# A fused pooled-attention and MLP kernel: three places of the first batch's order are changed

## The chip, the cores and the metric

The kernel runs on one core of a Trainium2 chip. The metric is the device time of one execution in microseconds (us); five runs of the kernel before are given, and their median is the time that a change is measured against. Beside it stands one execution taken by the hardware profiler, with its own time.

## The reference

Two stages are computed, one after the other. The first is attention over pooled keys and values (batch 8, heads 8, sequence 576, head size 64; eight neighbouring keys are averaged into one, so there are 72). The second is an MLP block with a mix over tokens in front.

```python
k_p = k.reshape(B, H, Sp, pool, D).mean(axis=3)        # pool = 8, Sp = 72
v_p = v.reshape(B, H, Sp, pool, D).mean(axis=3)
scores = scale * np.matmul(q, k_p.transpose(0, 1, 3, 2))
attn = softmax(scores)
x = np.matmul(attn, v_p)                               # then heads side by side: (8, 576, 512)

a1 = alpha1 * x + beta1
tok = np.einsum('ts,bsd->btd', w_tok, a1)
u = x + lam * tok
a2 = alpha2 * u + beta2
ch = np.maximum(a2 @ w_ch1, 0.0) @ w_ch2               # 512 -> 2048 -> 512
out = u + lam * ch
```

## The kernel before, in words

Each batch passes through attention (`att_...`), the token mix (`mix_T`, `mix_uT`) and the MLP (`mlp_A`, `mlp_B`). From the second batch on, attention of batch b+1 is interleaved with the MLP of a block of four 128-token chunks by due times that are sorted in a loop (L712 to L747). The first batch has nothing to lie beside: its attention is written out by hand from L583 to L662, and this is the stretch that the change touches. Every engine carries out its own instructions in the order in which the program issues them, so a line's place in this list is its place in its engine's queue.

The first batch in order:

- `keep_warm(4)` (L584) runs four matmuls on a constant tile ahead of everything else on TensorE. Two `broadcast`s (L267) spread lam and lam*alpha1 over the partitions; ScalarE copies them out (L586, L588).
- `cast_q` (L130), `att_F` (L369, L373): q is cast to bf16, transposed on TensorE and copied out. q and k come in two halves u of four heads, and the last 64 of the 576 tokens of all heads ("the rest") come in a tile of their own, `rem_raw`.
- `sum_k` (L138, L139) adds up k in three steps; the fourth level of the pooling is in a matmul. `cast_rem` (L121, L123, L124) casts the rest of q and adds up the rest of k into `rem_k`; before, all three instructions are on GpSimd. Its third argument, `copy`, gives the engine of the cast alone.
- `row_of_xs` (L273) writes one row of 512 products beta1*lam into `xs`, the right operand of the token mix: a bias row. It is one VectorE instruction on one partition. Only the fifth chunk of the mix's sum reads that row.
- `att_K` (L401, L404, L408): pooled keys by matmul, the third of them from `rem_k`, then two copies into `kpT`. `att_S` (L453, L455): scores of one head and their exponentials. `sum_v` (L416, L418), `att_V` (L424, L428): the same for v.
- `att_AV(0, h)` (L470 to L477): product of one head on TensorE; VectorE takes the reciprocal of the row sums and writes `x_tm`. `att_X` (L484, L488) multiplies two heads of `x_tm` by lam*alpha1 into `xs`, on GpSimd for the first six heads and on VectorE for the last two.
- In between the heads, `setup_wtok(c)` (L288, L291) transposes one column block of w_tok by five matmuls and ScalarE copies it into `wtT`; `setup_rowsum(c)` (L300, L302) sums its rows by five matmuls, and ScalarE copies one row. `setup_vectors` (L278) and `keep_warm(2)` follow.
- `mix_T(0, 0)` (L512) is the first product of the token mix. It reads all 512 columns of `xs`, so it follows all eight heads. After it TensorE has the mix and the MLP.

There are six PSUM buffers in turn for nearly all of TensorE's results (`gp`), and two more for the broadcasts and the MLP's sums. The loads are issued on SyncE's queue in the order q, k, rests, q, k, rest of v, v; w_tok and the MLP's weights are issued from GpSimd's queue, where `load_wtok` (L147, L149) and `load_w1` (L324) stand behind `cast_q(0, 1)` and the rest of v. The loads of the second batch are held back by a VectorE memset (L82) behind head 5's product, and GpSimd's part of v (`sum_v(0, 1)`) is held back by a memset (L613) that follows VectorE's `v_sum`.

Of the kernel before, what the change touches and what calls it, by code (L numbers as in the profile page):

```python
# [23 lines left out]
def kernel(  # L24
# [18 lines left out]
    nc = tc.nc  # L43
# [8 lines left out]
    def gp(name):  # L52
        return psA.tile([P, 512], FP, tag="gp", name=name)
# [10 lines left out]
    def keep_warm(count):  # L64

        ps = gp("ps_warm")
        for _ in range(count):
            nc.tensor.matmul(out=ps, lhsT=warm[:, 0:P], rhs=warm)
# [4 lines left out]
    def new_batch(b):  # L73
        st1[b] = {"qT": {}, "ET": [None] * H, "raw": [None] * 2, "q": [None] * 2,
                  "k": [None] * 2, "v": [None] * 2}
# [41 lines left out]
    def cast_rem(b, eng, copy=None):  # L117
        raw = st1[b]["rem_raw"]
        rq = work.tile([P, 4, D], BF, tag="rem_q", bufs=2, name="rem_q")
        rk = work.tile([P, 2, D], BF, tag="rem_k", bufs=2, name="rem_k")  # L120
        (copy or eng.tensor_copy)(out=rq, in_=raw[:, 0])  # L121
        t = raw[:, 1]
        eng.tensor_tensor(out=t[:, 0:2], in0=t[:, 0:2], in1=t[:, 2:4], op=ALU.add)  # L123
        eng.tensor_tensor(out=rk, in0=t[:, 0:1].to_broadcast((P, 2, D)),  # L124
                          in1=t[:, 1:2].to_broadcast((P, 2, D)), op=ALU.add)
        st1[b]["rem"] = rq, rk

    def cast_q(b, u, copy):
        bf = work.tile([P, 16, D], BF, tag="q_bf", bufs=3, name="q_bf")
        copy(out=bf, in_=st1[b]["raw"][u][:, 0].rearrange("p e j d -> p (e j) d"))  # L130
        st1[b]["q"][u] = bf

    def sum_k(b, u, eng):

        t = st1[b]["raw"][u][:, 1]
        bf = work.tile([P, 2, 2, D], BF, tag="k_bf", bufs=4, name="k_bf")
        for n in (4, 2):
            eng.tensor_tensor(out=t[:, :, 0:n], in0=t[:, :, 0:n], in1=t[:, :, n:2 * n], op=ALU.add)  # L138
        eng.tensor_tensor(out=bf, in0=t[:, :, 0:1].to_broadcast((P, 2, 2, D)),  # L139
                          in1=t[:, :, 1:2].to_broadcast((P, 2, 2, D)), op=ALU.add)  # L140
        st1[b]["k"][u] = bf
# [122 lines left out]
    def broadcast(i):  # L264

        ps = psB.tile([P, DM], FP, tag="ch", bufs=2, name="ps_bc")
        nc.tensor.matmul(out=ps, lhsT=ones_row, rhs=vecs[0:1, i])  # L267
        return ps

    def row_of_xs(i, eng):  # L270

        p0 = 64 - 64 * i
        eng.tensor_tensor(out=xs_pool[i][p0:p0 + 1, 4, :], in0=vecs[p0:p0 + 1, 2],  # L273
                          in1=vecs[p0:p0 + 1, 0], op=ALU.mult)
# [6 lines left out]
    def setup_wtok(tcx, copy):  # L281

        trc = P if tcx < 4 else REM
        w = wt_bf[0:trc, S * tcx:S * tcx + 640]
        strided = w[:, 0:512].rearrange("p (m c) -> p c m", c=4)
        ps_w = gp("ps_w").bitcast(BF)
        for sc in range(5):
            nc.tensor.transpose(out=ps_w[0:P, trc * sc:trc * sc + trc],  # L288
                                in_=strided[:, sc, :] if sc < 4 else w[:, 512:640],
                                identity=identity_bf[0:trc, 0:trc])  # L290
        copy(out=wtT[:, 0:5, P * tcx:P * tcx + trc],  # L291
             in_=ps_w[:, 0:5 * trc].rearrange("p (s t) -> p s t", t=trc))
# [84 lines left out]
    def att_Frem(b, us, copy):  # L377

        st = st1[b]
        if "ps_qr" not in st:  # L380
            ps_q = gp("ps_qr").bitcast(BF)
            ps_q = ps_q[:, 0:256].rearrange("p (a m) -> p a m", a=2)
            for a in range(2):
                nc.tensor.transpose(out=ps_q[:, a],
                                    in_=st["rem"][0][:, 2 * a:2 * a + 2].rearrange(
                                        "p j d -> p (j d)"),
                                    identity=identity_bf)
            st["ps_qr"] = ps_q
        for u in us:
            copy(out=qT_of(b, u)[:, :, 256:288].rearrange("p h (i a) -> p h i a", a=2),  # L390
                 in_=st["ps_qr"].rearrange("p a (i h) -> p h i a", h=8)[:, 4 * u:4 * u + 4])

    def att_K(b, u, *copies):

        st = st1[b]
        ps_kp = gp("ps_kp")


        kp = ps_kp[:, 0:320].rearrange("p (r h y) -> p r h y", r=2, h=2)
        for e in range(2):  # L400
            nc.tensor.matmul(out=kp[:, :, :, 8 + 32 * e:40 + 32 * e],  # L401
                             lhsT=st["k"][u][:, e].rearrange("p t d -> p (t d)"), rhs=sel_k)
        kp = ps_kp[:, 0:320].rearrange("p (r y) -> p r y", r=2)
        nc.tensor.matmul(out=kp[:, :, 72:88], lhsT=st["rem"][1].rearrange("p t d -> p (t d)"),  # L404
                         rhs=pool_rem[:, 4 * u:4 * u + 4])
        for j in range(2):
            rows = slice(64 * j, 64 * j + 64)
            copies[j % len(copies)](  # L408
                out=kpT_pool[u][rows, j].rearrange("p r (h x) -> p r h x", h=2)[:, :, :, 0:72],
                in_=kp[rows, :, 8:152].rearrange("p r (h x) -> p r h x", h=2))  # L410
# [35 lines left out]
    def att_S(b, h):  # L446

        st = st1[b]
        u, r, hh = h // 4, h // 2 % 2, h % 2
        ET, n = ET_pool[(8 * b + h) % 6], P if hh else SPG  # L450
        for j in range(2):
            ps_sc = gp("ps_sc")
            nc.tensor.matmul(out=ps_sc[0:n, 0:288], lhsT=kpT_pool[u][:, j, r, 72 * hh:72 * hh + n],  # L453
                             rhs=st["qT"][u][:, h % 4, :])
            nc.scalar.activation(out=ET[0:n, 64 + j:64 + S + j:2], in_=ps_sc[0:n, 0:288],  # L455
                                 func=AF.Exp, bias=0.0, scale=1.0 / 64)
        st["ET"][h] = ET

    def att_AV(b, h):
        st = st1[b]  # L460
        if "x" not in st:
            st["x"] = work.tile([P, 5, DM], FP, tag="x_tm", bufs=1, name="x_tm")
        hp, hh = h // 2, h % 2
        n = P if hh else SPG
        ET, vp1, x = st["ET"][h][0:n], vp1_pool[b % 2][hh][0:n, hp], st["x"]
        ps_av = gp("ps_av")
        av = ps_av[:, 0:5 * 66].rearrange("p (c x) -> p c x", x=66)
        for c in range(4):
            m0 = 64 + 256 * (c // 2) + c % 2
            nc.tensor.matmul(out=av[:, c, :], lhsT=ET[:, m0:m0 + 256:2], rhs=vp1)  # L470

        r0 = 576 - 64 * (b % 2)
        nc.tensor.matmul(out=av[:, 4, :], lhsT=ET[:, r0:r0 + 128], rhs=vp1)  # L473
        rec = work.tile([P, 5], FP, tag="rec", bufs=2, name="rec")
        nc.vector.reciprocal(out=rec, in_=av[:, :, 64:65])  # L475
        dd = D * h
        nc.vector.tensor_tensor(out=x[:, :, dd:dd + D], in0=av[:, :, 0:64],  # L477
                                in1=rec.unsqueeze(2).to_broadcast((P, 5, D)), op=ALU.mult)

    def att_X(b, h0, h1, eng=nc.vector):  # L480

        x, xs = st1[b]["x"], xs_pool[b % 2]
        cols = slice(D * h0, D * h1)
        eng.tensor_tensor(  # L484
            out=xs[:, 0:4, cols], in0=x[:, 0:4, cols],
            in1=lamal_bc[:, cols].unsqueeze(1).to_broadcast((P, 4, D * (h1 - h0))), op=ALU.mult)
        p0 = 64 * (b % 2)
        eng.tensor_tensor(out=xs[p0:p0 + 64, 4, cols], in0=x[p0:p0 + 64, 4, cols],  # L488
                          in1=lamal_bc[p0:p0 + 64, cols], op=ALU.mult)
# [91 lines left out]


    new_batch(1)  # L583
    keep_warm(4)  # L584
    ps_lam = broadcast(0)
    nc.scalar.copy(out=lam_bc, in_=ps_lam)  # L586
    ps_lamal = broadcast(1)
# [2 lines left out]
    att_F(0, 0)  # L590
    fill_E()
    sum_k(0, 0, nc.vector)
    cast_rem(0, nc.gpsimd)
    cast_q(0, 1, nc.gpsimd.tensor_copy)
    row_of_xs(0, nc.vector)
    att_Frem(0, (0,), nc.scalar.copy)
    att_K(0, 0, nc.vector.tensor_copy, nc.scalar.copy)
    att_Frem(0, (1,), nc.vector.tensor_copy)
# [7 lines left out]
    att_F(0, 1)  # L606
    att_S(0, 2)
    att_K(0, 1, nc.vector.tensor_copy)
    att_S(0, 3)
    v_00 = st1[0]["v"][0]  # L610
    sum_v(0, 0)
# [23 lines left out]
    load_v(1, 0)  # L635
    load_v(1, 1)
    att_X(0, 4, 6, nc.gpsimd)
    setup_wtok(2, nc.scalar.copy)
    att_AV(0, 6)
    setup_rowsum(0)  # L640
    setup_rowsum(1)
    setup_wtok(3, nc.scalar.copy)
    att_AV(0, 7)
    att_X(0, 6, 8)
    setup_rowsum(2)
    setup_rowsum(3)
# [131 lines left out]
```

The softmax here doesn't subtract the row's maximum and nothing guards it: scores larger than these inputs give would overflow.

## Time and profile before

| | |
|---|---|
| median of 5 runs | 370.13 us (370.0 to 371.06) |
| profiled execution | 370.5 us, of which the span from first to last instruction is 368.7 us |
| TensorE busy | 357.1 us, 97% of the span |
| VectorE, ScalarE, GpSimd busy | 218.4, 214.1, 126.2 us |
| chain of waits by engine | TensorE 91%, ScalarE 3%, DMA 2%, VectorE 1% |
| first product of the token mix starts | 25.34 us after the span's start |

In the profile PE is TensorE's matmul, PEld its weight load, DVE VectorE, ACT ScalarE, POOL GpSimd, and SP the engine that issues most of the loads. In the timeline a row gives start and duration in us, then engine, line, operation, output <- inputs, shape and count, and in brackets the idle time before it and what ended it. The chain of waits goes back from the last instruction to whatever released it, step by step; it is the list of what had to be done one after another. A queue's name with a q behind it (SPq) means that the engine issues a transfer.

### The profile page before, as it was taken

To read this page: it belongs to the slowest core of one execution; us is meant where nothing else is said; L and a number is where in the kernel's file an instruction comes from. 1 tells how busy PE (TensorE), PEld (TensorE's weight loads), DVE (VectorE), ACT (ScalarE), POOL (GpSimd) and SP (SyncE) were. 2 spreads that over 40 slices of the span, in tenths; PEclk is the share of its full clock that TensorE was granted. 3 is DMA by queue.
4 is the path that set the end of the run, shared out by engine and by line. 5 is a ranking of instruction groups with operands and counts; after the bars stand their busy time and mean duration, and the time that the engine had idled before them with its cause. 6 is when DMAs were issued, how large, how long until landed. Compare 5 with 4: busy or idle time off the path is not lost.

```text
span 368.7 us, 6142 instructions
## 1 busy us (share of the span) xinstructions
PE 357.1 (97%) x2304; PEld 197.9 (54%) x2346; DVE 218.4 (59%) x437; ACT 214.1 (58%) x420; POOL 126.2 (34%) x182
## 2 busy tenths in 40 slices
PE   7799999999999999999999999999999999999995
PEld 2477655455545554555455555555455545544544
DVE  7765544883786368734876387727863687543011
ACT  3855984389527970698158923895279705712710
POOL 7857813072507231542227140905072410000000
PEclk9999999999999999999999999999999999999999
DMA  7999993039012901192107402470100002002002
GB/s 241 274 232 322 245 296 106 24 127 349 30 42 85 341 16 51 57 306 80 59 28 254 162 30 57 159 256 30 56 30 2 29 31 57 2 28 85 2 28 85
DMA packets 19575, 43.27 MB, mean 117 GB/s; under 512 B 2193, under 2 KB 4565, under 8 KB 19546
## 3 DMA queue, kind: packets, MB, share of 16 engines
q1 hardware_dynamic: 17488, 37.89, 29.9%
q0 software_dynamic: 1888, 4.86, 6.8%
q8 instruction: 18, 0.29, 0.3%
q10 hardware_dynamic: 170, 0.14, 0.2%
q14 instruction: 11, 0.09, 0.1%
HBM read 38.30 MB, written 9.44 MB: 129 GB/s over the span
## 4 chain that ended last, share of the span: by engine, by line
PE 91%; ACT 3%; DMA 2%; DVE 1%; issue 1%; SPq 1%
PE ps_ch L566 33%; PE ps_h L543 32%; PE ps_tok L512 12%; PE ps_sc L453 4%; PE ps_av L470 2%; PE ps_uT L527 2%; DMA qk_raw<-in_k_dram 2%; ACT Hj L548 2%; PE ps_q L369 1%; PE ps_w L288 1%; SPq L84 1%; PE ps_av L473 1%; PE ps_kp L401 1%; PE ps_rs L300 0%; ACT qT L373 0%
## 5 line engine op out<-in xcount | busy, mean ns | idle before, releaser
L543 PE MATMUL ps_h<-u_fm,w 128*128 128x512 bf16 (+1 forms) x575 | 133.7, 373 | 1.4 <-ACT u_fm L529 0.4
L566 PE MATMUL ps_ch<-w,Hj 128*128 128x512 bf16 x489 | 123.9, 379 | 1.3 <-issue 0.2
L548 ACT ACTIVATE Hj<-ps_h,bias_cols 128x512 bf16<-128x512 f32 x144 | 97.1, 691 | 34.0 <-PE ps_h L543 33.5
L543 PEld LDWEIGHTS <-w 128*128 128x128 bf16 x592 | 64.1, 114 | 48.3 <-issue 0.6
L566 PEld LDWEIGHTS <-Hj 128*128 128x128 bf16 x592 | 55.6, 98 | 49.1 <-issue 0.2
L529 ACT COPY u_fm<-ps_uT 128x512 bf16<-128x512 bf16 x36 | 21.1, 588 | 80.5 <-PE ps_uT L527 80.4
L484 POOL TENSOR_TENSOR xs<-x_tm,lamal_bc 128x512 bf16<-128x512 f32 x24 | 30.5, 1272 | 82.3 <-DVE x_tm L477 82.3
L455 ACT ACTIVATE ET<-ps_sc 128x288 f16<-128x288 f32 (+1 forms) x128 | 51.6, 488 | 11.1 <-PE ps_sc L453 10.6
L512 PE MATMUL ps_tok<-xs,wtT 128*128 128x512 bf16 (+1 forms) x200 | 49.3, 379 | 0.1
L573 DVE TENSOR_TENSOR u_sb<-u_sb,ps_ch 128x512 f32<-128x512 f32 (+1 forms) x37 | 24.9, 673 | 24.9 <-PE ps_ch L566 23.8
L408 DVE CAST kpT<-ps_kp 64x288 bf16<-64x288 f32 x31 | 14.1, 455 | 40.3 <-PE ps_kp L404 40.0
L572 DVE TENSOR_TENSOR ps_ch<-lam_bc,ps_ch 128x512 f32<-128x512 f32 x32 | 22.2, 693 | 24.9 <-PE ps_ch L566 24.8
L514 DVE TENSOR_TENSOR u_sb<-x_tm,ps_tok 128x512 f32<-128x512 f32 (+1 forms) x40 | 27.4, 685 | 13.0 <-PE ps_tok L512 12.8
L477 DVE TENSOR_TENSOR x_tm<-ps_av,rec 128x320 f32<-128x320 f32 x64 | 31.5, 492 | 2.7
L475 DVE RECIPROCAL rec<-ps_av 128x5 f32<-128x5 f32 x64 | 12.3, 193 | 34.6 <-PE ps_av L473 34.4
L512 PEld LDWEIGHTS <-wtT 128*128 128x128 bf16 (+1 forms) x200 | 18.8, 98 | 23.4 <-DVE xs L484 2.0
L453 PE MATMUL ps_sc<-qT,kpT 128*128 128x288 bf16 (+1 forms) x128 | 29.3, 306 | 0.9 <-DVE kpT L408 0.8
L138 POOL TENSOR_TENSOR qk_raw<-qk_raw 128x512 f32<-128x512 f32 (+1 forms) x28 | 29.7, 1060 | 1.1
L516 DVE TENSOR_TENSOR u_bf<-u_sb,al_bc 128x512 bf16<-128x512 f32 (+1 forms) x39 | 27.3, 700 | 1.4
L671 POOL COPY ticks<-ticks 1x1 f32<-1x1 f32 x6 | 1.1, 178 | 73.4 <-DVE ticks L667 73.4
L470 PEld LDWEIGHTS <-ET 72*128 72x128 f16 (+1 forms) x256 | 17.1, 102 | 14.1 <-DVE vp L428 0.6
L416 DVE TENSOR_TENSOR v_u<-v_u 128x512 f32<-128x512 f32 (+1 forms) x30 | 23.5, 783 | 0.8
(115 smaller groups left out, 324.6 us busy)
## 6 DMA issues: line engine op xcount, KB each, us to landing
qk_raw<-in_q_dram SPq DMA_DIRECT2D x16, 512.0 KB, 7.1
qk_raw<-in_k_dram SPq DMA_DIRECT2D x16, 512.0 KB, 6.6
v_u<-in_v_dram SPq DMA_DIRECT2D x32, 256.0 KB, 7.2
out_dram<-u_sb SPq DMA_DIRECT2D x32, 256.0 KB, 2.3
w<-in_moe_w_ch_dram POOLq DMA_DIRECT2D x2, 1024.0 KB, 13.8
w<-in_moe_w_ch_dram POOLq DMA_DIRECT2D x4, 512.0 KB, 10.7
rem_raw<-in_q_dram SPq DMA_DIRECT2D x8, 128.0 KB, 4.7
rem_raw<-in_k_dram SPq DMA_DIRECT2D x8, 128.0 KB, 5.2
```

The lines of the kernel that those rows point to most:

```text
L138: eng.tensor_tensor(out=t[:, :, 0:n], in0=t[:, :, 0:n], in1=t[:, :, n:2 * n], op=ALU.add)
L453: nc.tensor.matmul(out=ps_sc[0:n, 0:288], lhsT=kpT_pool[u][:, j, r, 72 * hh:72 * hh + n], rhs=st["qT"][u][:, h % 4, :])
L455: nc.scalar.activation(out=ET[0:n, 64 + j:64 + S + j:2], in_=ps_sc[0:n, 0:288], func=AF.Exp, bias=0.0, scale=1.0 / 64)
L477: nc.vector.tensor_tensor(out=x[:, :, dd:dd + D], in0=av[:, :, 0:64], in1=rec.unsqueeze(2).to_broadcast((P, 5, D)), op=ALU.mult)
L484: eng.tensor_tensor(out=xs[:, 0:4, cols], in0=x[:, 0:4, cols], in1=lamal_bc[:, cols].unsqueeze(1).to_broadcast((P, 4, D * (h1 - h0))), op= ...
L512: nc.tensor.matmul(out=ps_tok, lhsT=wtT[0:kk, at, t0:t0 + P], rhs=xs[0:kk, sc, :], start=(sc == 0), stop=(sc == 4))
L514: nc.vector.tensor_tensor(out=s["u"][p0:p1, :], in0=st1[b]["x"][p0:p1, c, :], in1=ps_tok[p0:p1, 0:DM], op=ALU.add)
L516: eng.tensor_tensor(out=s["u_bf"][p0:p1, :], in0=s["u"][p0:p1, :], in1=al2_bc[p0:p1, :], op=ALU.mult)
L543: nc.tensor.matmul(out=ps_h[:, t0:t1], lhsT=w1_of(cc, j), rhs=u_fm[n][:, cc, t0:t1], start=(cc == 0), stop=(cc == 3))
L548: nc.scalar.activation(out=t, in_=ps_h, func=AF.Relu, bias=bias_cols[:, j:j + 1], scale=1.0)
L566: nc.tensor.matmul(out=ps, lhsT=Hj[n, j][:, 128 * m:128 * m + 128], rhs=w2_of(n, j, cols), start=(j == 0), stop=(j == NJ - 1))
L573: nc.vector.tensor_tensor(out=u, in0=u, in1=ps, op=ALU.add)
```

## The change

Four edits in the list of the first batch. `keep_warm(4)` at the start goes. `cast_rem(0)` keeps GpSimd for the cast of q's rest, and VectorE takes the two additions of k's rest, behind `sum_k(0, 0)`. `row_of_xs(0)` leaves its place ahead of the first half's `att_K` and goes behind the second half's, ahead of `sum_v(0, 0)`. The product of head 6 goes ahead of the transposes of w_tok's block 2, and that of head 7 goes ahead of two row sums and the transposes of block 3.

```diff
     new_batch(1)
-    keep_warm(4)
     ps_lam = broadcast(0)
...
     fill_E()
     sum_k(0, 0, nc.vector)
-    cast_rem(0, nc.gpsimd)
+    cast_rem(0, nc.vector, nc.gpsimd.tensor_copy)
     cast_q(0, 1, nc.gpsimd.tensor_copy)
-    row_of_xs(0, nc.vector)
     att_Frem(0, (0,), nc.scalar.copy)
     att_K(0, 0, nc.vector.tensor_copy, nc.scalar.copy)
...
     att_K(0, 1, nc.vector.tensor_copy)
+    row_of_xs(0, nc.vector)
     att_S(0, 3)
     v_00 = st1[0]["v"][0]
     sum_v(0, 0)
...
     att_X(0, 4, 6, nc.gpsimd)
+    att_AV(0, 6)
     setup_wtok(2, nc.scalar.copy)
-    att_AV(0, 6)
+    att_AV(0, 7)
     setup_rowsum(0)
     setup_rowsum(1)
     setup_wtok(3, nc.scalar.copy)
-    att_AV(0, 7)
     att_X(0, 6, 8)
     setup_rowsum(2)
     setup_rowsum(3)
```

## The prediction

> **What bounds the kernel now.** I read the page first, then the chain of waits of the first 40 us, then each engine's timeline there.
>
> ```profile
> PE 357.1 (97%) x2304; PEld 197.9 (54%) x2346; DVE 218.4 (59%) x437; ACT 214.1 (58%) x420; POOL 126.2 (34%) x182
> PE   7799999999999999999999999999999999999995
> PEclk9999999999999999999999999999999999999999
> ```
>
> TensorE is busy in all slices but the first two and the last, so after some 20 us a delay at the start is not won back, and a gain at the start is kept. The change touches only those first 26 us. The chain of waits there (start, us, what):
>
> ```profile
> 4.39 6.85 DMA qk_raw<-in_k_dram
> ...
> 12.45 0.84 DVE k_bf L139
> ...
> 13.34 0.39 PE ps_kp L401 x2
> ...
> 14.27 0.46 DVE kpT L408
> ...
> 14.77 0.70 DVE v_u L416
> ...
> 15.95 0.30 DVE v_sum L418
> ...
> 16.30 0.30 PE ps_v L424
> ...
> 16.62 0.29 DVE vp L428
> ...
> 16.96 0.40 PE ps_av L470 x4
> ...
> 23.56 0.70 ACT wtT L291
> ...
> 24.30 0.44 PE ps_rs L300 x5
> ...
> 24.89 0.32 PE ps_warm L68
> ...
> 25.34 3.41 PE ps_tok L512 x15
> ```
>
> Three parts are to be seen. Up to 11.24 the second k transfer decides. From there to 16.96 it is VectorE, back to back: k's sum, k's copies, v's sum, v's copy. From 16.96 to 25.34 it is TensorE, with one stop at the end, where the row sum of block 3 waits for ScalarE's copy of that block. The mix starts at 25.34; what this start gains or loses I carry to the end of the kernel, since no wait on a transfer stands between 11.3 and 60 us in the list of waits, by which the loss could be swallowed.
>
> The rows of VectorE and GpSimd that I use for costs:
>
> ```profile
> 9.16 0.83 DVE L273 TENSOR_TENSOR xs<-vecs 1x512 bf16<-1x512 f32 x1
> 10.02 0.45 DVE L408 CAST kpT<-ps_kp 64x288 bf16<-64x288 f32 x1
> 24.51 0.69 DVE L484 TENSOR_TENSOR xs<-x_tm,lamal_bc 128x512 bf16<-128x512 f32 x1
> 25.12 0.28 DVE L488 TENSOR_TENSOR xs<-x_tm,lamal_bc 64x128 bf16<-64x128 f32 x1
> 9.41 1.48 POOL L130 CAST q_bf<-qk_raw 128x1024 bf16<-128x1024 f32 x1
> ```
>
> **The change part by part.**
>
> *The bias row behind k's copies.* At its old place the row (9.16 to 9.99) stands in the gap that ends with the transfer: VectorE idles 0.60 us before 11.26. Its new place is between k's last copy (ends 14.73) and v's sum (14.77), where VectorE has no gap. All of it goes on the chain. Cost, start to start: an elementwise product of 512 columns with an independent one behind it takes 25.12 - 24.51 = 0.61 us (L484 to L488). Lower bound 0.55 (L262, one partition, 4.71 to the next start at 5.26), upper bound 0.83 (the row itself at 9.16, beside GpSimd's work). At 14.8 GpSimd issues weight loads (13.93 to 15.48) and reads no tile, so I take 0.61. Behind it wait v's sum, the matmul L424, GpSimd's memset L613 and with it the second half of v, and all products: +0.61. The loads of batch 1 (memset L82, then eleven issues on SP's queue) come 0.61 later too; their first user, GpSimd's cast at 31.27, starts without a wait behind its own work, which has moved as far.
>
> *Rests of k on VectorE.* Two additions (L123, L124) of 128 columns leave GpSimd (0.51 each) and stand behind `k_bf` (ends 9.13). A VectorE sum with such an output takes 0.29 (L418 at 15.95). Two dependent ones: 9.15 + 0.31 + 0.31, so `rem_k` is there at about 9.75 instead of 9.43; the matmul L404 takes 0.21 (9.49 to 9.70 before), so k's first copy can start at 10.02. Before, it started at 10.02 as well, held not by the matmul but by the bias row on VectorE. So one delay takes another's place: 0. GpSimd disturbs this, though. Its cast of q's second half (1.48) moves up to 1.02 earlier, if that q has landed, and may run beside the two sums. The row at 9.16 shows what that does: L273 took 0.83 beside this cast against 0.61 alone (L262), +0.21. The page "SBUF — State Buffer" of the Trainium skill, section "Who interferes with whom", says more: a VectorE instruction with two SBUF inputs and a GpSimd instruction that reads SBUF exclude each other for a whole instruction. By that the sums could wait 1.48 for the cast, and k's first copy would be at about 11.4. I keep to the row: up to +0.2 for each sum. The cover is thin: TensorE's work behind that copy ends at 13.22, and the second `att_K` starts at 13.34, so 0.12 us of lateness is free and the rest counts. Between -0.12 (GpSimd's rest-of-v sums, also earlier, leave the 0.83 of L139 at 12.45 undisturbed, which gains only until TensorE is free) and +0.3; I take 0.
>
> *GpSimd's queue.* Behind the cast are two issues of w_tok, three sums of v's rest and two issues of w1; they move earlier by at most 1.02 and then stop at the memset L613, which waits for v's sum in either order. w_tok takes 6.9 us to land from 10.83, and TensorE asks for it at 19.07 without waiting: no gain. Earlier packets could push the k transfer that ends at 11.24: at most about 0.2, taken as 0 since the cast likely waits for its own q.
>
> *`keep_warm(4)`.* Four loads and four matmuls of 0.43 start to start (2.19 to 4.01). The broadcasts behind them may start up to 1.8 us sooner, but the second waits for VectorE's product (ends 5.32), and the first scores wait for k's copy at 10.02 in any case: 0. Does the clock need them? The granted clock reads 1.00 in every slice, but the durations say otherwise:
>
> ```profile
> 7.72 1.03 PE L369 MATMUL ps_q<-identity_bf,q_bf 128*128 128x128 bf16 x8
> 35.82 0.61 PE L369 MATMUL ps_q<-identity_bf,q_bf 128*128 128x128 bf16 x8
> ```
>
> Eight equal transposes go at half speed at 7.72, right behind the warm matmuls and broadcasts; the rows turn fast at about 23.3. The page "TensorE: Matmul & The Clock Gate", section "Part 1: The HAM clock gate", says that the clock opens after a busy window of about 3.4 us, with windows that run freely. That rule speaks against the edit: less early work could keep the clock shut, and one window more at half speed costs up to 1.7 us. The trace shows the clock shut with them, too, so by the row they are worth 0, and I take 0.
>
> *The last heads' products ahead.* TensorE's order becomes head 6, block 2, head 7, row sums 0 and 1, block 3, row sums 2 and 3. The work is the same, but its tail is not. Before, head 7's product lay in the shadow of ScalarE's copy of block 3 (transposes end 23.53, copy 23.56 to 24.26, row sum 3 at 24.30). Ahead of block 3 it delays the transposes, so the copy, row sum 3, the vector, two warm matmuls and the mix. Its time is 0.24 (23.31 to 23.55, fast clock) to 0.29 (21.44 to 21.73, head 6, slow): +0.25. What it gains is `xs` on VectorE: head 7's chain from product to `xs` (23.75 to 25.20) ends more than 1 us sooner. But TensorE reached the mix at about 25.30 behind its own warm matmuls (two from 24.87, 0.215 each by the four in 0.86 of the MLP's rows; the records hold one of them), so `xs` was not the last: gain 0, at most 0.1. Head 6 and block 2 only change places: 0. Where ScalarE's copies of w_tok (back to back from 20.06 to 22.37) bind, the 0.25 is 0.
>
> The sum: 0.61 + 0.25 = +0.86 us. It is made in the profiled execution (370.5, its span 368.7 and 1.8 around it), which lies 0.37 above the median; I add it to the median: 370.13 + 0.86 = 370.99, that is 371.0. About 0.2%, or 0.74 us, is what a measurement of this kernel can tell from no change: 369.39 to 370.87 is "same".
>
> **The rivals.**
>
> *The clock opens when it did.* If it opens at 23.3 again, the work that the delay pushes behind 23.3 runs at double speed. Half of 0.61 comes back: +0.55, 370.7. For: the switch may depend on a free-running window. Against: the rule counts busy time, and the busy stretch itself starts 0.61 later.
>
> *The rests are late.* GpSimd's cast starts at 8.3 and both sums lose 0.2: k's first copy at 10.4, second `att_K` 0.25 late: 371.25, up to 371.5 if the k transfer suffers. For: L273's 0.83. Against: GpSimd took the cast at 9.41 right behind its sums, and the transfers' order (this q before the k that ends at 11.24) puts that q's landing near 9.3.
>
> *v's sum is not what TensorE waits for,* or the row costs nothing: only +0.25, 370.4. Against: matmul L424 starts 0.05 behind `v_sum`.
>
> *Faster: the clock opens a window sooner.* With a shifted start of the busy stretch the switch may fall near 19.9 instead of 23.3. TensorE's 3.4 us in between would take 1.7. With +0.86 that gives 370.13 - 0.84 = 369.29. It decides if TensorE alone binds there. Against: the pause before the products grows from 0.58 to 1.2 us, and ScalarE's copies bind from 20.06 to 22.37, so 1.7 is the most.
>
> **How the numbers follow.** The sum as worked out 0.50, of which 0.39 lies above 370.87 and 0.11 below; the clock as it was 0.22 (0.01 above); late rests 0.15, all slower; v's sum not last 0.05; the clock sooner 0.08. Slower 0.39 + 0.01 + 0.15 = 0.55; same 0.11 + 0.21 + 0.05 = 0.37; faster 0.08. The range leaves out most of the faster case and the end of the late rests: 369.5 to 371.9.
>
> **What would show it.** Right: L273 between k's last copy and L416, L416 starting near 15.4, the first product near 17.6, head 7's `xs` finished 0.5 us or more before the mix, the mix near 26.2, then the same distances to the end. The rests: L123 and L124 beside or ahead of the cast L130, k's first copy at 10.0. Wrong, if the first product starts by 17.1, if the mix starts before 25.5, if transposes at 7.7 to 20 have become fast, or if a transfer's wait stands behind 25 us.

## The result, and the profile after

| | before | changed | ratio, 95% interval |
|---|---|---|---|
| median of the runs | 370.19 us (42 runs) | 371.14 us (22 runs) | 1.0025 [1.0017, 1.0032] |
| profiled execution | 370.5 us | 371.39 us | |
| its span | 368.7 us | 369.6 us | |
| first product of the mix | 25.34 us | 26.20 us | |

The kernel is slower by 0.95 us in the medians. The mix starts 0.86 us later in the profile and the span is 0.9 us longer, so what the first batch loses stays lost to the end, as the first view of the page suggests: TensorE has no free slice behind the start.

```profile
PE 355.2 (96%) x2300; PEld 197.1 (53%) x2342; DVE 219.7 (59%) x439; ACT 214.1 (58%) x420; POOL 125.6 (34%) x180
PE   5699999999999999999999999999999999999995
PEclk9999999999999999999999999999999999999999
```

The chain of waits of the changed kernel up to the mix (start, us, what):

```profile
8.55 0.42 DVE k_bf L139
8.98 0.21 DVE rem_raw L123
...
9.21 1.02 DVE rem_k L124
...
10.52 0.46 DVE kpT L408
...
11.03 1.36 PE ps_sc L453 x4
12.39 0.85 PE ps_q L369 x8
13.24 0.48 PE ps_sc L453 x2
13.72 0.21 PE ps_kp L401 x2
...
14.48 0.46 DVE kpT L408
...
14.97 0.68 DVE xs L273
...
15.69 0.70 DVE v_u L416
...
16.87 0.30 DVE v_sum L418
...
17.89 0.40 PE ps_av L470 x4
...
24.21 0.26 ACT wtT L302
...
24.50 0.70 ACT wtT L291
...
25.24 0.44 PE ps_rs L300 x5
...
25.83 0.32 PE ps_warm L68
...
26.20 3.41 PE ps_tok L512 x15
```

Two things are new on it. Between k's second copy and v's sum stands the bias row: 0.68 long, and v's sum starts 0.72 behind the row's start. And the second k transfer is no longer on the chain at all; in its place stand the rest of k, which is there only at 10.23 instead of 9.43, and TensorE's scores and transposes behind k's first copy (10.52 instead of 10.02), which now end so late that the second `att_K` follows them without a gap.

Every profile of this case can be cut at the same four points: VectorE starts the second k sum (the transfer has landed), TensorE starts the second `att_K`, TensorE starts the first product, the mix starts. The last column says how long behind the first product TensorE's clock opened for the last time; the moment is taken from the list of granted clocks that each trace keeps (the last section has more on it).

| kernel | k sum starts | to att_K | to first product | to the mix | clock opens behind first product |
|---|---|---|---|---|---|
| before | 11.26 | 2.08 | 3.62 | 8.38 | 6.5 |
| changed | 11.09 | 2.43 | 4.37 | 8.31 | 6.0 |

Changed minus before: -0.17 + 0.35 + 0.75 - 0.07 = +0.86. The first term is the transfer's own scatter (10.99 to 12.30 in all profiles). The second is the rest of k, the third the bias row, the fourth the new order of the products together with a clock that opened 0.6 us nearer to the first product in this execution.

### The profile page after: what moved, and what is told of

It is laid out like the page before. It is cut to its first block, busy times and chain, and to the rows that moved or that the text cites. A ratio compares the mean times of both kernels' runs of the same rounds, so it can differ in the third digit from the quotient of the medians.

```text
span 369.6 us, 6135 instructions
## 1 busy us (share of the span) xinstructions
PE 355.2 (96%) x2300; PEld 197.1 (53%) x2342; DVE 219.7 (59%) x439; ACT 214.1 (58%) x420; POOL 125.6 (34%) x180
## 4 chain that ended last, share of the span: by engine, by line
PE 91%; ACT 3%; DVE 2%; issue 1%; DMA 1%; ACTq 0%; DVEq 0%
PE ps_ch L566 33%; PE ps_h L543 32%; PE ps_tok L512 12%; PE ps_sc L453 5%; PE ps_av L470 2%; PE ps_uT L527 2%; PE ps_q L369 2%; ACT Hj L548 2%; DMA vecs<-in_moe_alpha_dram 1%; PE ps_av L473 1%; PE ps_kp L401 0%; ACT qT L373 0%; PE ps_w L288 0%; PE ps_rs L300 0%; DVE qk_raw L138 0%
## 5 line engine op out<-in xcount | busy, mean ns | idle before, releaser
L484 POOL TENSOR_TENSOR xs<-x_tm,lamal_bc 128x512 bf16<-128x512 f32 x24 | 30.5, 1271 | 82.3 <-DVE x_tm L477 82.3
L416 DVE TENSOR_TENSOR v_u<-v_u 128x512 f32<-128x512 f32 (+1 forms) x30 | 23.5, 784 | 0.8
```

The lines of the kernel that those rows point to most:

```text
L484: eng.tensor_tensor(out=xs[:, 0:4, cols], in0=x[:, 0:4, cols], in1=lamal_bc[:, cols].unsqueeze(1).to_broadcast((P, 4, D * (h1 - h0))), op= ...
```

## The experiments

Each was timed in five rounds beside the kernel before on one chip, and profiled once. Four make one edit of the change alone in the kernel before; four alter the changed kernel; the last four build on what the first eight had shown. Times of different groups were taken on different chips, so each is judged by its ratio to the kernel before. This ratio is not the quotient of the two medians shown (s_rest: 0.16% by the ratio, 0.09% by the medians); a claim of an effect on the time needs an interval that leaves out 1.

| kernel | median us | before us | ratio, 95% interval | k sum starts | to att_K | to first product | to the mix | clock opens |
|---|---|---|---|---|---|---|---|---|
| s_row | 370.69 | 369.94 | 1.0015 [1.0007, 1.0023] | 11.66 | 2.21 | 4.35 | 7.66 | 4.6 |
| s_rest | 370.26 | 369.94 | 1.0016 [1.0005, 1.0027] | 11.34 | 2.31 | 3.60 | 8.76 | 7.5 |
| s_products | 370.29 | 369.94 | 1.0008 [0.9995, 1.0021] | 11.23 | 2.18 | 3.63 | 8.50 | 6.5 |
| s_warm | 370.16 | 369.94 | 1.0002 [0.9990, 1.0014] | 12.12 | 2.11 | 3.57 | 7.33 | 3.9 |
| u_rowlate | 370.11 | 369.95 | 1.0010 [0.9999, 1.0020] | 12.30 | 2.08 | 3.64 | 8.45 | 6.4 |
| u_hold | 370.31 | 369.95 | 1.0013 [1.0004, 1.0021] | 10.99 | 2.22 | 4.34 | 8.45 | 6.4 |
| u_products | 370.24 | 369.95 | 1.0014 [1.0005, 1.0022] | 11.57 | 2.08 | 4.34 | 8.08 | 5.8 |
| u_row_hold | 369.34 | 369.95 | 0.9989 [0.9977, 1.0000] | 11.29 | 2.14 | 3.63 | 8.13 | 5.6 |
| b_fill | 369.77 | 369.88 | 0.9997 [0.9986, 1.0007] | 11.08 | 2.23 | 3.63 | 7.27 | 1.9 |
| u_split | 369.56 | 369.88 | 0.9989 [0.9977, 1.0000] | 11.14 | 2.08 | 3.01 | 7.81 | 4.6 |
| u_split_fill | 369.12 | 369.88 | 0.9981 [0.9973, 0.9989] | 11.25 | 2.08 | 3.23 | 7.18 | 2.4 |
| u_row_hold2 | 369.82 | 369.88 | 1.0000 [0.9989, 1.0010] | 11.27 | 2.08 | 3.63 | 7.78 | 4.7 |

The table shows at once what a single profile can and can't say. The column "to first product" has two values, 3.6 and 4.35, as long as VectorE makes both of k's last copies, and the bias row alone decides which; only u_split and u_split_fill, which give one copy to ScalarE, come below. The column "to the mix" runs from 7.18 to 8.76 and follows the last column: it is mostly TensorE's clock. So a mix that starts sooner in one profile proves nothing before the clock is looked at.

### One edit alone

**s_row**, the bias row behind k's copies:

```diff
-    row_of_xs(0, nc.vector)
     att_Frem(0, (0,), nc.scalar.copy)
...
     att_K(0, 1, nc.vector.tensor_copy)
+    row_of_xs(0, nc.vector)
```

> The kernel before with one edit: the bias row moves behind the copies of k's second half. Theory (the row lies whole on VectorE's chain to the first product): L273 takes 0.68 to 0.72 start to start, k's first copy comes at about 9.75 instead of 10.02 without use, since the second k sum still ends at 13.29; v's sum starts near 15.45, the first product near 17.65, the mix 0.6 to 0.7 later than 25.34; time +0.6 to +0.7 us. Rival (v's sum is not what TensorE waits for): first product at 17.0 to 17.1, time within 0.1 us. Rival (the clock opens at the same moment, so half comes back): first product near 17.65, mix only 0.3 to 0.4 later.

Measured: L273 takes 0.68, the first product comes 4.35 behind the second `att_K` instead of 3.62 (+0.73), time +0.15%, some 0.56 us (0.75 by the medians). VectorE's timeline of this kernel:

```profile
14.33 0.94 DVE L408 CAST kpT<-ps_kp 64x288 bf16<-64x288 f32 x2 [0.52 <-PE ps_kp L404]
15.30 0.68 DVE L273 TENSOR_TENSOR xs<-vecs 1x512 bf16<-1x512 f32 x1
16.02 1.15 DVE L416 TENSOR_TENSOR v_u<-v_u 128x512 f32<-128x512 f32 x2
```

No gap on either side of the row: it is on the chain. The rival by which v's sum isn't waited for falls. The mix itself came at 25.88 because the clock opened early in this execution; the times, which average over many, keep most of the loss.

**s_rest**, the rest of k on VectorE:

```diff
-    cast_rem(0, nc.gpsimd)
+    cast_rem(0, nc.vector, nc.gpsimd.tensor_copy)
```

> The kernel before with one edit: VectorE adds up the rest of k, the bias row stays ahead of k's first copy. Theory A (VectorE's sum with two SBUF inputs waits until GpSimd's cast of q is over): L124 ends 0.1 to 0.2 after the cast, near 10.2, the row follows, k's first copy near 10.85, the second att_K on TensorE near 13.9 instead of 13.34, mix and time +0.5 us. Theory B (the two only slow each other, 0.2 for an instruction, as the prediction took it): L124 at most 0.5 long, k's first copy near 10.4, second att_K near 13.5, time +0.1 to +0.2 us.

Measured: +0.16% (0.59 us; 0.32 by the medians), the second `att_K` 2.31 behind the start of k's sum instead of 2.08, and k's first copy at 10.66. The instruction that got long is this time the first of the two sums. VectorE's and GpSimd's timelines:

```profile
8.47 1.12 DVE L123 TENSOR_TENSOR rem_raw<-rem_raw 128x128 f32<-128x128 f32 x1
9.62 0.29 DVE L124 TENSOR_TENSOR rem_k<-rem_raw 128x128 bf16<-128x128 f32 x1
8.36 1.09 POOL L130 CAST q_bf<-qk_raw 128x1024 bf16<-128x1024 f32 x1
```

The cast runs from 8.36 to 9.45; the sum that started inside it ends at 9.59, 0.14 behind the cast, and the next one takes its 0.29. In the changed kernel it was L124, again 0.14 behind the cast (10.22 and 10.08):

```profile
9.21 1.01 DVE L124 TENSOR_TENSOR rem_k<-rem_raw 128x128 bf16<-128x128 f32 x1
8.94 1.14 POOL L130 CAST q_bf<-qk_raw 128x1024 bf16<-128x1024 f32 x1 [0.70 <-DMA qk_raw<-in_q_dram]
```

That is theory A, though its moments came sooner than expected, because q landed sooner here (the cast started at 8.36). The delay of `att_K` in this profile, 0.23, is less than half of the 0.5 expected, since TensorE's gap ahead of it takes up a part; 0.53 more was lost later in this execution to GpSimd's half of v, which TensorE awaited at 19.8.

**s_products**, heads 6 and 7 ahead (the last part of the change's diff, alone):

> The kernel before with one edit: the products of heads 6 and 7 go ahead. Theory (head 7's product loses its cover behind ScalarE's copy of block 3): the first product stays at 16.96, block 3's copy starts 0.25 later than 23.56, the last row sums 0.25 later than 24.30, the mix at 25.5 (of the 0.25, 0.08 comes back because xs is no longer last), time +0.1 to +0.2 us. Rival (the early xs is what counts): mix at 25.26 or sooner, time -0.1 us. Where the clock opens at another moment than 23.3 in this profile, the copy's start moves by half of that difference, and the row sums must be judged by their distance from block 3's transposes.

Measured: the first product 3.63 behind `att_K`. Time +0.08% with an interval from -0.05% to +0.21%: the direction is not told by the times. The profile tells it better, since its clock opened at the same distance as that of the kernel before (6.54 and 6.53). The last row sums start 7.53 behind the first product instead of 7.34, and the mix 8.50 instead of 8.38: 0.19 are lost and 0.07 come back, where 0.25 and 0.08 were expected. More profiles with like clocks are put together under u_products.

**s_warm**, without the four matmuls at the start (the first line of the change's diff, alone):

> The kernel before without the four first matmuls. Theory: no step of the chain moves; first product 16.96, mix 25.34 within 0.1 us, time within 0.15 us. Rival (they help to open TensorE's clock): the fast rows begin later than 23.3, mix up to 1.7 us later.

Measured: 1.0002 [0.9990, 1.0014], and the steps up to the first product are those of before (2.11 and 3.57). The clock opened earlier here, not later. Nothing is seen to hang on these four matmuls.

The four ratios add up to +0.41%, that of the whole change is +0.25%. Each single interval reaches 0.08 to 0.13% to either side, so the times alone do not tell whether the parts simply add up.

### One thing changed in the changed kernel

**u_rowlate**, the row behind VectorE's last `xs`:

```diff
     att_K(0, 1, nc.vector.tensor_copy)
-    row_of_xs(0, nc.vector)
...
     att_X(0, 6, 8)
+    row_of_xs(0, nc.vector)
```

> The changed kernel with one edit: the bias row goes far back, behind VectorE's last xs, where VectorE has more than 1 us to spare. Theory (the row is on the chain where the change put it): v's sum starts near 14.97, the first product near 17.17, mix 0.6 to 0.7 sooner than 26.20, time 0.6 to 0.7 us under the changed kernel, 370.4 to 370.5. Rival (clock gives back half): mix 0.35 sooner, time 370.8.

Measured: 3.64 to the first product instead of 4.37, so the whole 0.73 is back, and the ratio is 1.0010 instead of 1.0025 (0.55 us less, where 0.6 to 0.7 were expected; the two were taken on different chips). The first product came at 18.02, not 17.17, because the transfer of k landed at 12.30 in this execution; with it q came late, GpSimd's cast started at 10.82 behind both sums, and L123 and L124 took 0.28 and 0.29. That is theory A of s_rest once more, found without an edit: where the cast doesn't meet the sums, they are short.

**u_hold**, the cast waits for the rest of k:

```diff
     cast_rem(0, nc.vector, nc.gpsimd.tensor_copy)
+    held = const.tile([1, 1], BF, tag="held", name="held")
+    nc.gpsimd.tensor_copy(out=held, in_=st1[0]["rem"][1][0:1, 0, 0:1])
     cast_q(0, 1, nc.gpsimd.tensor_copy)
```

> The changed kernel with GpSimd's cast of q's second half held back until VectorE has summed the rest of k (a copy of one element from rem_k ahead of the cast). Theory (lock: L124 waited for the cast): L124 takes 0.3 instead of 1.01, k's first copy near 9.9 instead of 10.52, the second att_K on TensorE near 13.3 instead of 13.52, mix and time 0.2 us sooner, near 370.95. Rival (L124 is slow by itself or waits for something else): L124 stays near 1.0, no difference.

```profile
8.79 0.29 DVE L124 TENSOR_TENSOR rem_k<-rem_raw 128x128 bf16<-128x128 f32 x1
9.38 0.45 DVE L408 CAST kpT<-ps_kp 64x288 bf16<-64x288 f32 x1 [0.30 <-PE ps_kp L404]
9.27 1.03 POOL L130 CAST q_bf<-qk_raw 128x1024 bf16<-128x1024 f32 x1
```

Measured: L124 takes 0.29, k's first copy comes 0.30 behind it, `att_K` 2.22 behind the start of k's sum instead of 2.43. The cast, undisturbed, takes 1.03, where it took 1.48 in the kernel before: there it had been waiting as well. Time 1.0013, 0.44 us under the changed kernel by the ratios, with intervals that overlap; the expected 0.2 is within them.

**u_products**, the products back in their old places:

> The changed kernel with the products of heads 6 and 7 back in their old places. Theory (the order of the products costs 0.25 and saves 0.08): the last row sums start 0.25 sooner behind the first product at the same clock, mix 0.1 to 0.25 sooner than 26.20, time near 371.0. Rival (the new order pays): mix 0.1 or more later.

Measured: mix at 26.07, time 1.0014. By the ratios that is 0.41 us under the changed kernel, more than the profiles account for, with intervals that overlap. The order is judged by pairs of profiles whose clocks open at nearly the same distance from the first product:

| clock opens | old order, to the mix | new order, to the mix | difference |
|---|---|---|---|
| 6.5 and 6.5 | before 8.38 | s_products 8.50 | +0.12 |
| 6.5 and 6.4 | before 8.38 | u_hold, u_rowlate 8.45 | +0.07 |
| 5.8 and 5.6 | u_products 8.08 | u_row_hold 8.13 | +0.05 |
| 4.6 and 4.7 | s_row 7.66 | u_row_hold2 7.78 | +0.12 |

In the old order the stretch grows by some 0.37 for each us by which the clock opens later (7.66 at 4.58, 8.38 at 6.53). With the small differences within the pairs taken out by that slope, the new order costs 0.09 to 0.13 us in all four, where 0.17 to 0.25 were expected. The early `xs` is there: the last L484 starts at 24.16 in the changed kernel, with 2.04 us left to the mix, against 24.51 and 0.83 before. It buys next to nothing, because TensorE is still behind its own row sums:

```profile
23.96 0.44 PE L288 MATMUL ps_w<-identity_bf,wt_bf 128*128 128x128 bf16 x5
24.24 0.39 PE L300 MATMUL ps_rs<-wtT,ones_bf 128*128 128x128 bf16 x4
25.24 0.38 PE L300 MATMUL ps_rs<-wtT,ones_bf 128*128 128x128 bf16 x4 [0.56 <-ACT wtT L291]
24.16 0.85 DVE L484 TENSOR_TENSOR xs<-x_tm,lamal_bc 128x512 bf16<-128x512 f32 x1
```

TensorE waits 0.56 for ScalarE's copy of block 3 here (0.31 before, 0.50 in s_products), which is mostly head 7's missing cover. In this execution ScalarE's copy of a row sum (L302) also stands on the chain, just ahead of the copy of block 3; in the kernel before and in s_products that copy follows the transposes directly.

**u_row_hold**, both u_rowlate and u_hold:

> The changed kernel with both: the bias row behind VectorE's last xs, and the cast held back until the rest of k is summed. Theory (two separate delays that add up): first product near 16.95, mix 0.85 to 0.9 sooner than 26.20, time 370.2 to 370.3, as the kernel before. Rival (one hides the other): no better than the row alone, 370.4 or more.

Measured: 2.14, 3.63, 8.13, mix at 25.19, as the kernel before within the scatter; the two delays add up. The time was 0.9989 [0.9977, 1.0000], a little better than expected; run again in the next group (u_row_hold2) it was 1.0000.

### Towards a better order

**b_fill**, two more constant matmuls in TensorE's gaps of the kernel before:

```diff
     att_S(0, 5)
+    ps_fill = psB.tile([P, DM], FP, tag="ch", bufs=2, name="ps_fill")
+    nc.tensor.matmul(out=ps_fill, lhsT=warm[:, 0:P], rhs=warm)
     att_V(0, 0, nc.vector.tensor_copy)
+    nc.tensor.matmul(out=ps_fill, lhsT=warm[:, 0:P], rhs=warm)
     att_AV(0, 0)
```

> The kernel before with two more matmuls on the constant tile, 512 columns each, into a PSUM buffer that nothing else needs then: one in TensorE's gap ahead of v's matmul L424 (idle 0.58), one in the gap ahead of the first product (idle 0.38). Theory (the opening of TensorE's clock follows an unbroken busy stretch): first product within 0.1 of 3.62 us behind the second att_K; the clock opens earlier than the 4.5 to 6.5 us behind the first product that the runs so far show, by 1 us or more, the stretch from first product to mix is under 8.0 instead of 8.38; time 0.3 to 0.6 us under the kernel before. Rival (the two short gaps do not matter to the clock): stretch 8.1 to 8.5, time within 0.2 us or slower by the 0.05 to 0.1 that a fill may overlap the work behind it.

Measured: in the profile the clock opened 1.9 behind the first product, the earliest of all, the stretch was 7.27 and the span 367.6. The times say 0.9997 [0.9986, 1.0007]: no gain in the average. The granted clocks of the single runs show that the fills do act on the clock. Profiles in which the clock opened early and closed again have a mean granted clock of 0.991 to 0.995, the others 0.998 to 1.000. Of the 48 runs of the kernel before in this group, 21 have 0.995 or less; of the 14 of b_fill and the 19 of u_split_fill none. But those 21 runs are no slower than the rest (369.77 in the median against 370.11), so keeping the clock from closing again gains little; b_fill's slowest run is 370.39, against 371.12 for the kernel before.

**u_split**, u_row_hold with k's last copy on ScalarE:

```diff
-    att_K(0, 1, nc.vector.tensor_copy)
+    att_K(0, 1, nc.vector.tensor_copy, nc.scalar.copy)
```

> The changed kernel with the row behind VectorE's last xs and the cast held back (as u_row_hold), and the second copy of k's second half given to ScalarE. Theory (VectorE's chain from k's sum to the first product is what TensorE waits for, instruction by instruction): one copy of 0.48 start to start leaves the chain, v's sum 0.48 sooner; the first product 3.15 to 3.3 us behind the second att_K instead of 3.63 (the scores of head 5 may bind ahead of it); time 0.3 to 0.45 us under u_row_hold. Rival (ScalarE's exponentials, now 0.4 later, are waited for instead): gain under 0.15 us.

Measured: 3.01 to the first product instead of 3.63, more than the 0.48 of one copy: v's sum starts 0.37 behind the start of the copy that is left (13.68 to 14.05), where it started 0.98 behind the first of two (13.79 to 14.77). But ScalarE comes onto the chain of waits:

```profile
14.16 0.39 ACT kpT L408
...
15.43 0.37 ACT vp L444
...
16.21 1.17 ACT ET L455 x3
...
17.42 0.38 PE ps_av L470 x4
```

ScalarE's copy of k, its exponentials and its small copies of v now stand one behind another, and the third head's product follows the exponentials. So the rival holds in part. Time 0.9989 against 1.0000 of u_row_hold2 beside it, 0.26 us by the medians, less than expected and with overlapping intervals; that ScalarE takes up the rest of the 0.6 is likely, but not shown.

**u_split_fill**, both:

> u_split with the two matmuls of b_fill. Theory: both add up, 0.3 to 0.6 us under u_split where the clock opens earlier; the gaps are smaller here, so a fill of 0.43 can push the first product by up to 0.3. Rival: the fills only push, time 0.1 to 0.3 us over u_split.

Measured: 369.12 us, 0.9981 [0.9973, 0.9989]: faster than the kernel before by 0.7 us, and the only one whose interval says so. The first product comes 0.22 later behind `att_K` than in u_split, as the fills push, and the stretch to the mix is 7.18. This is the version that beats both kernels. Which part the fills have in it is not settled: 0.44 us lie between the medians of u_split and this one, but the two intervals overlap.

**u_row_hold2**, u_row_hold again:

> u_row_hold once more, beside the three others on one chip. Theory: the row costs nothing where it lies now and the rests nothing without the cast beside them, so the time is that of the kernel before within 0.3 us; a gain of 0.3 us or more again would say that the edits together are worth something that the single ones did not show.

Measured: 1.0000 [0.9989, 1.0010]; the gain of u_row_hold did not come again. The changed kernel without its two delays is worth what the kernel before is worth.

## Why the prediction was right, point by point

The time was forecast as 371.0 (+0.86) and is 371.14 (+0.95). Sum and sign are right; three of the terms have other sizes, and their errors cancel in part. The forecast terms were 0.61, 0 and 0.25. In the profiles they are 0.73, then 0.23 to 0.35 where the cast meets the sums, and about 0.1: together 1.06 to 1.18. The mechanism of the largest term is right; that the sum lies within 0.1 of the measured time is in part luck. Why the times show 0.95 and not more is argued, not shown: where q lands late, the rests cost nothing.

*The bias row: 0.61 forecast, 0.72 measured* from its start to v's sum (0.75 in the changed kernel's steps, 0.73 in s_row and u_rowlate). The mechanism is as told. The size was taken from L484 and the start behind it, with inputs on 128 partitions. The row itself takes 0.68 when nothing disturbs it, and that length was not in the profile before, where it stood beside GpSimd (0.83); both bounds held it.

*The rests of k: 0 forecast, with a range from -0.12 to +0.3; +0.35 measured between k's sum and `att_K` in the changed kernel, +0.23 in s_rest, 0 where q lands late.* Here the step failed by which the row at 9.16 was set against the skill's rule. L273's 0.83 was read as a slowing beside the cast. But the cast starts behind the row (9.41 and 9.16), and what already ran when the row started was GpSimd's second addition, in the kernel before:

```profile
8.92 0.51 POOL L124 TENSOR_TENSOR rem_k<-rem_raw 128x128 bf16<-128x128 f32 x1
```

It ends at 9.43; the row ends 0.56 behind it, which is its own 0.68 less 0.12; and the cast ends at 10.89, 0.90 behind the row, which is its own 1.03 less 0.13. So each waited for the one that had started first, and this row is a case of the rule, not evidence against it. The runs show the rule of the Trainium skill's page "SBUF — State Buffer", section "Who interferes with whom": a sum with two SBUF inputs that starts inside GpSimd's cast ends 0.14 behind the cast's end, three times out of three (changed, s_rest, u_products, where L124 took 1.03), and takes 0.29 when the cast is held back. The figure worked out from the rule was too dark (copy at 11.4, measured 10.52) because it was made with the 1.48 of before: undisturbed the cast takes 1.03, and 0.27 of it were over when L124 started. The forecast's rival "the rests are late" was thus part of what happened, near its price of 0.25 but by another mechanism than the 0.2 for each sum: one sum waited and the other did not.

*The products ahead: +0.25 forecast, less at most 0.1 for the early `xs`; +0.09 to +0.13 measured at like clocks.* Head 7 does lose its cover (TensorE's wait for the copy grows from 0.31 to 0.56). In s_products, with the clock at the same distance, the last row sums come 0.19 later and not 0.25: the chain has block 3's transposes at 0.47 there against 0.55 before, since the clock opens while they run (23.58). Head 7's 0.24, read as a duration at the fast clock, likewise has the opening in it (23.49). Then 0.07 come back ahead of the mix; in the changed kernel the gap between the warm matmuls and the mix is 0.05 on the chain, 0.13 before.

*`keep_warm(4)`: 0 forecast, 1.0002 measured.* The four matmuls had neither a part in the chain nor, as far as s_warm shows, in the clock.

*The rival "the clock opens when it did"* asked whether the opening moves with the busy stretch or stays at 23.3. In the profiles it does neither: it comes from 1.9 to 7.5 us behind the first product, and scatters from one execution to the next (the last section shows what it goes by). The 0.6 us by which the changed kernel's clock was nearer to the first product hid some 0.2 of the other terms in that one profile (at 0.37 for each us).

*The rival by which the clock opens a window sooner* is seen in single runs. Of the changed kernel's 22 runs, 8 have a granted clock of 0.990 to 0.995, as the profiles in which it opened early and closed again; their median is 370.5, that of the others 371.4. But the kernel before has such runs too (21 of 48 in the last group), so it is not the change that makes them.

*GpSimd's queue* moved as told and gained nothing: the cast waited for its own q (0.70 idle ahead of 8.94), so w_tok's issue came only 0.8 sooner.

## What to carry to other kernels

An instruction that "fits behind" another has to be set against the engine's own timeline: if the engine has no gap there, its whole start-to-start time goes on the chain, however small it looks, and a place with slack (here 0.6 us ahead of a transfer, or 1 us at the end of the stretch) costs nothing. Before work is moved between VectorE and GpSimd, lay the two timelines over each other: a sum with two SBUF inputs that started inside GpSimd's cast ended 0.14 us behind the cast here, and was short when it did not. An instruction that looks slow beside another must be set against what had started before it. And where a stage's length changes between profiles, cut it at fixed points and look at the clock first, by durations as well; only pieces between the same points, at the same clock, can be subtracted.

## What the runs showed of the hardware that was not expected

The clock column can be blind until the first change. In the kernel before it says 1.00 from the start, though transposes go at half speed until about 23.5. The list of granted clocks that the trace keeps begins with the first change (at 23.49 in the kernel before), and the column shows what lies ahead of it as 1.00. In s_rest the clock opened early and closed again, and from then on the column tells the truth. Its windows (from:to, length, PE busy, PEclk, DMA share, GB/s):

```profile
16.00:17.00 1.00, 0.23 (x1) 1.00 0.99 166
17.00:18.00 1.00, 0.75 (x12) 0.96 1.03 179
18.00:19.00 1.00, 1.00 (x13) 0.50 1.20 223
...
24.00:25.00 1.00, 1.00 (x14) 0.62 1.15 223
25.00:26.00 1.00, 1.00 (x8) 1.00 1.10 205
```

TensorE's rows of the same kernel show where it had opened, and that the column missed the slow time before:

```profile
13.65 0.42 PE L401 MATMUL ps_kp<-sel_k,k_bf 128*128 128x128 bf16 x2
14.48 0.30 PE L442 MATMUL ps_v<-vrem,sel_rem 128*128 128x66 f16 x4
17.25 0.30 PE L470 MATMUL ps_av<-vp,ET 72*128 72x66 f16 x4 [0.38 <-DVE vp L428]
18.04 0.42 PE L470 MATMUL ps_av<-vp,ET 72*128 72x66 f16 x4
```

The two products are alike and take 0.30 and 0.42; the clock was open from about 14.5. Half-microsecond windows of s_warm give the moments more closely:

```profile
18.00:18.50 0.50, 0.50 (x11) 0.79 0.96 174
...
21.50:22.00 0.50, 0.50 (x13) 0.80 1.10 209
```

A mean of 0.79 over 0.5 us is 0.29 at full and 0.21 at half speed, so the clock closed at 18.29; by the same count it opened at 21.70, 3.41 us later. In s_rest it closed at 17.93 and opened at 24.76, 6.83 or twice 3.41 later; in u_split at 17.45 and 20.87. This agrees with the freely running windows of about 3.4 us that the Trainium skill's page "TensorE: Matmul & The Clock Gate", section "Part 1: The HAM clock gate", describes. The lists bear it out over the whole run: every interval between two changes, in all 14 profiles, is 3.413, 6.827, 344.746 or 348.159 us long, that is 1, 2, 101 or 102 times 3.4133. The clock closed although TensorE was at work for much of the window before (2.12 of 3.41 us in s_rest).

With the windows known, each can be looked at by itself. The two ahead of the opening in the kernel before, and the one in b_fill:

```profile
16.66:20.08 3.42, 3.12 (x35) 1.00 1.11 205
20.08:23.49 3.41, 3.41 (x43) 1.00 1.12 212
15.40:18.82 3.42, 3.27 (x25) 1.00 1.08 193
```

In all 14 profiles the window that ends with the last opening is one in which TensorE was busy nearly throughout: 3.27 in b_fill, over 3.36 in the others. The window ahead of it never had more than 3.13 (s_products). So the pauses around the first product decide which window can open the clock, and where the windows happen to lie in an execution decides the rest. The two kernels with filled pauses have the earliest openings (1.9 and 2.4 us behind the first product), which fits; of their times only u_split_fill's are clearly better. Busy time is not the whole rule, though: the clock opened early behind windows of 2.81 (u_split, 10.63 to 14.04) and 3.02 (s_warm, 11.46 to 14.87), and it stayed shut behind a full one (before, 3.01 to 6.42). What else counts stays open.

The stretch from the first product to the mix runs from 7.18 to 8.76 us, and most of the difference goes with this moment: about 1.6 us between these profiles, more than any edit of this case is worth.
